# Seven block products for half of the last block's tails, and a copy moved to VectorE

## The chip, the cores and the metric

The kernel runs on one NeuronCore of a Trainium2 chip. The metric is the device time of one execution in microseconds (us). Before the change it was 275.11 us, the median of three runs (275.05 to 275.95). About 0.3% (0.8 us) is what a measurement of this kernel can tell from no change.

Engines: TensorE (PE in the profile, its weight loads PEld), VectorE (DVE), ScalarE (ACT), GpSimd (POOL), SyncE (SP, which only issues DMAs here). Each runs its own queue strictly in order and waits on semaphores for the others.

## The reference

Linear attention with cosine weights, then a two-layer network with a sigmoid-approximated gelu. For 8 batches of 8 heads, 576 positions and 64 features:

```
phi(x)  = [relu(x) * cos(pos), relu(x) * sin(pos)]
kv      = phi(k)^T v ;  z = sum over positions of phi(k)
attn    = (phi(q) kv) / (phi(q) z + 1e-6)
x       = attn as 4608 tokens of 512
h       = x @ w_in            (512 x 2048)
g       = h / (1 + exp(-1.702 h))
out     = g @ w_out           (2048 x 512)
```

Inputs and output are float32; the kernel computes the products in bf16 with sums in float32.

## The kernel before, in words

**Blocks and tails.** A batch has 576 tokens: a block of 512 and a tail of 64. The kernel runs batch by batch over the blocks; the tails' tokens are gathered in the tile `xt` (4 chunks of 128 features by 8 x 64 tokens). Batch 0's tail goes through the first product early (`mm1_tail_first`, result in `gt0`). The other seven tails, 448 tokens, are left for the last block, b = 7.

**The first product (x @ w_in)** has 16 groups of 128 hidden features, here numbered fc 0 to 15. Written plainly, one group is four matmuls (four chunks of features) into one PSUM bank and one gelu on ScalarE from that bank to SBUF. For the tails this is `mm1_tails` (L393 to L400): 64 matmuls of 448 columns, 16 gelus, the four banks of the pool `pmm` taken in turn. The gelu writes to `gt5`, the tile `gt` seen as 16 groups by 2 halves by 8 batches by 32 tokens: the first 32 tokens of every tail form one column half, the second 32 the other.

**Seven products for eight.** The larger products use the scheme of Strassen in Winograd's form: cut both matrices into 2 x 2 blocks, make a few sums of blocks, and do seven block products instead of eight. It is used twice.

- For the first product, a `Unit` (L643 to L695) does four groups fc (2u, 2u+1, 8+2u, 8+2u+1) for two column halves. It has seven steps, each of 4 matmuls: 1, 2, 6, 7, 5, 4, 3 in this order. Steps 1, 6, 7 and 4 add up in one bank (A), step 2 uses a second (Bk), steps 5 and 3 a third (Bp). After steps 1, 6 and 7 ScalarE copies bank A out to SBUF ("snap": s1, s2, s3, L672). VectorE adds such a copy to a bank (L667): c11 = s1 + step 2, c22 = s3 + step 5, c12 = s2 + (step 5 + step 3). Step 3 may only be added onto its bank when c22 has read it. Each of c11, c22, c12 and the end state of bank A gets a gelu on ScalarE.
- Weight sums (`win_sum`, L618 to L627: s1 to s4, in two halves of 512 columns each, "window sums" below, 128 x 1024 each) and x sums (`x_sum`, L632 to L641: t1, t2, t3, nt4) are made on VectorE ahead.
- For the second product (g @ w_out), `wino_mm` does the seven products of 16 matmuls each; the sums of g are made on VectorE by `g_sums` (L466 to L479), called "tail sums" when they are of the tails: s1 and s2 for two halves, then s3 and s4 for two halves, eight of 128 x 1024.

In blocks 2 to 6 a pair of units does half of the first product in the middle of seven plain groups (`mm1_pair`).

**The last block's order** (L1040 to L1113) is written out by hand, there is no scheduler; an engine's queue holds the instructions in the order in which the code emits them:

1. GpSimd: the copy of `gt0` into column 0 of `gt5` (L1041), then eight output DMAs that had been put off (`later`, L1043).
2. TensorE and ScalarE: `mm1_tails` for fc 0 to 15. VectorE meanwhile: eight window sums, four x sums.
3. VectorE: the tail sums s1, s2.
4. TensorE: four main units (the first product of block 7), with the 14 halves of the tails' second product between their steps: step 1 of unit 0, a half, step 2, a half, step 6, step 1 of unit 1, and so on. VectorE emits the tail sums s3, s4 after unit 0's c11.
5. The main block's second product, and its output.

The functions that the change touches and what calls them, with the line numbers of the profile:

Of the kernel before, what the change touches and what calls it, by code (L numbers as in the profile page):

```python
# [9 lines left out]
F32 = mybir.dt.float32  # L10
BF16 = mybir.dt.bfloat16
AF = mybir.ActivationFunctionType
# [3 lines left out]
SUB = mybir.AluOpType.subtract  # L16
# [4 lines left out]
def kernel(  # L21
# [9 lines left out]
    nc = tc.nc  # L31
    B, H, S, D = q.shape
# [3 lines left out]
    FC = d_ff // 128  # L36
    NS = S // 64
    MT = 512
# [8 lines left out]
    pmm = ctx.enter_context(tc.tile_pool(name="pmm", bufs=4, space=PSUM))  # L47
    pat = ctx.enter_context(tc.tile_pool(name="pat", bufs=2, space=PSUM))
# [61 lines left out]
    vt = one.tile([128, NS, NI, VW], BF16, name="vt")  # L110
# [257 lines left out]
    def gelu(fc, units=False):  # L368
        if fc % 4 == 0 and not units:
            gT[fc // 4] = gpool.tile([128, 4, MT], BF16, name="g")  # L370
        nc.scalar.activation(gT[fc // 4][:, fc % 4], hp.pop(fc), AF.Gelu_apprx_sigmoid)  # L371
# [18 lines left out]
                                 start=(kc == 0), stop=(kc == KC - 1))  # L390
        nc.scalar.activation(gt0[:, ts(half, 8)], hps, AF.Gelu_apprx_sigmoid)

    def mm1_tails(fc):  # L393
        hps = pmm.tile([128, MT], F32, name="mm")
        for kc in range(KC):
            nc.tensor.matmul(hps[:, 64:B * 64], wcol(kc, fc), xt[:, kc, 64:B * 64],  # L396
                             start=(kc == 0), stop=(kc == KC - 1))
        nc.scalar.activation(gt5[:, fc, :, 1:B].rearrange("p a b t -> p b a t"),
                             hps[:, 64:B * 64].rearrange("p (b a t) -> p b a t", a=2, t=32),
                             AF.Gelu_apprx_sigmoid)  # L400
# [210 lines left out]
    def slot():  # L611
        slot_no[0] += 1
        return slots[slot_no[0] % 8].rearrange("p (f t) -> p f t", f=2)

    def win_sum(n, i, ws=ws):
        tt = nc.vector.tensor_tensor
        o = {m: ws[m][:, :, ts(i, 512)] for m in ws}
        a = {(0, k): w_in_t[i][:, ts(k, 2), :] for k in range(2)}  # L618
        a.update({(1, k): w_in_t[2][:, ts(k, 2), ts(i, 512)] for k in range(2)})
        if n == "s1":  # L620
            tt(o[n], a[1, 0], a[1, 1], op=ADD)
        elif n == "s2":
            tt(o[n], o["s1"], a[0, 0], op=SUB)
        elif n == "s3":
            tt(o[n], a[0, 0], a[1, 0], op=SUB)
        else:
            tt(o[n], a[0, 1], o["s2"], op=SUB)  # L627

    def x_blk(b, k, t):
        return x[b][:, ts(k, 2), ts(t, 256)]  # L630

    def x_sum(b, n, xs=xs):  # L632
        tt = nc.vector.tensor_tensor
        if n == "t1":
            tt(xs[n], x_blk(b, 0, 1), x_blk(b, 0, 0), op=SUB)
        elif n == "t2":
            tt(xs[n], x_blk(b, 1, 1), xs["t1"], op=SUB)
        elif n == "t3":
            tt(xs[n], x_blk(b, 1, 1), x_blk(b, 0, 1), op=SUB)
        else:  # L640
            tt(xs[n], x_blk(b, 1, 0), xs["t2"], op=SUB)  # L641

    class Unit:  # L643
        def __init__(self, b, u, A, Bk, Bp, ws=ws, xs=xs, slot=slot):
            self.b, self.u, self.ws, self.xs, self.slot = b, u, ws, xs, slot
            self.A, self.Bk, self.Bp = [t.rearrange("p (f t) -> p f t", f=2) for t in (A, Bk, Bp)]

        def mm(self, to, a, t, opens):
            for j in range(2):
                fc = 2 * self.u + j  # L650
                for k in range(2):
                    if isinstance(a, str):
                        lhs = self.ws[a][:, k, ts(fc // 4, 512)].rearrange("p (f c) -> p f c", c=4)[:, :, fc % 4]
                    else:
                        lhs = wcol(2 * a[1] + k, 8 * a[0] + fc)
                    rhs = self.xs[t][:, k] if isinstance(t, str) else x_blk(self.b, *t)[:, k]

                    nc.tensor.matmul(to[:, j], lhs, rhs, start=(opens and j == 0 and k == 0), stop=(k == 1),  # L658
                                     skip_group_check=True)

        def gelu(self, f, t, i):
            o = gT[2 * f + self.u // 2][:, ds(2 * (self.u % 2), 2), ts(t, 256)]
# [12 lines left out]
        def step(self, p):  # L675
            if p == 1:
                self.mm(self.A, (0, 0), (0, 0), True)
                self.s1 = self.snap(self.A)
            elif p == 2:
                self.mm(self.Bk, (0, 1), (1, 0), True)  # L680
                self.c11 = self.add(self.s1, self.Bk)
            elif p == 6:
                self.mm(self.A, "s2", "t2", False)
                self.s2 = self.snap(self.A)
            elif p == 7:
                self.mm(self.A, "s3", "t3", False)
                self.s3 = self.snap(self.A)
            elif p == 5:
                self.mm(self.Bp, "s1", "t1", True)
                self.c22 = self.add(self.s3, self.Bp)  # L690
            elif p == 4:
                self.mm(self.A, (1, 1), "nt4", False)
            else:
                self.mm(self.Bp, "s4", (1, 1), False)
                self.c12 = self.add(self.s2, self.Bp)  # L695

# [13 lines left out]
    def x_pair(b):  # L712
        t = xpool.tile([128, KC, MT], BF16, name="xT")
        xp[b] = {n: t[:, i].rearrange("p (k t) -> p k t", k=2) for i, n in enumerate(("t1", "t2", "t3", "nt4"))}
        for n in xp[b]:
            x_sum(b, n, xp[b])
# [256 lines left out]
    for b in range(1, B):  # L973
        nb = b + 1 if b + 1 < B else None
        if nb is None:
            break
        f0 = 5 if b == 1 else 0
        if b in PAIR:
            mm1_pair(b, nb)
        for fc in range(f0, FC) if b not in PAIR else ():  # L980
            if b == 1 and fc == f0:
                for c in range(5):
                    trig_q(c)
                    qturn_dma(c)
            if nb is not None and fc == f0 + 1:
                kv_operands(nb)

                if nb + 1 < B:
                    load(kf, k, nb + 1, nc.sync)
                    load_q(nb + 1, nc.sync)  # L990
            if fc == 8 and b == 1:
                vcopy()
            if fc == 12:
                g_sums(("s1", "s2"), 0)
            mm1(b, fc)
        if nb is not None:
            x_open(nb)
            if b == 1:
                kv_mm_next()
            g_sums(("s1", "s2"), 1)  # L1000
            if b > 1:
                x_next(nb, 0)
            if b == 1:
                kv_evac(0, 4)
                g_sums(("s3",), 0)
            at = ({2: [0], 3: [1], 4: [2], 6: [3], 8: [4]} if b == 1 else
                  {s: [p + 1 if nb < B - 1 else (4, 1, 2, 3)[p]] for p, s in enumerate((1, 3, 4, 6))})
            wino_open()
            for p in range(7):
                for c in range(2):  # L1010
                    wino_mm(p, c)
                    s = 2 * p + c
                    if c == 1:
                        wino_after(b, p)
                    for c2 in at.get(s, ()):
                        x_next(nb, c2)
                        if c2 == 3 and nb + 1 < B:
                            load(vf, v, nb + 1, nc.sync)

                    s0 = 4 if b > 2 else 8  # L1020
                    if s0 <= s < s0 + 5 and nb + 1 < B:
                        trig_q(s - s0, act=True)
                    if 8 <= s < 13 and nb + 1 < B:
                        qturn_dma(s - 8)
                    if s == 4 and b > 1:
                        for n in ("s3", "s4"):
                            g_sums((n,), 0)
                            g_sums((n,), 1)
                    if s == 2 and b == 1:
                        g_sums(("s3",), 1)  # L1030
                    if s == 4 and b == 1:
                        g_sums(("s4",), 0)
                    if s == 6 and b == 1:
                        g_sums(("s4",), 1)
            if nb in PAIR:
                x_pair(nb)

    b = B - 1  # L1040
    nc.gpsimd.tensor_copy(gt5[:, :, :, 0], gt0.rearrange("p f (a t) -> p f a t", a=2))  # L1041
    for o, i in later:
        nc.gpsimd.dma_start(out=o, in_=i)  # L1043
    for fc in range(FC):
        mm1_tails(fc)
        if fc == 0:
            for n in ("s1", "s2", "s3", "s4"):
                for i in range(2):
                    win_sum(n, i)
            for n in ("t1", "t2", "t3", "nt4"):  # L1050
                x_sum(b, n)
    for h in range(2):
        g_sums(("s1", "s2"), h, TAIL)
    two = [pat.tile([128, 2, 512], F32, name="at") for _ in range(2)]
# [89 lines left out]
```

## Time and profile before

| what | value |
|---|---|
| median of three runs | 275.11 us |
| the profiled execution: time, span | 275.49 us, 273.4 us |
| granted TensorE clock | 0.998 |
| stage 2, tails' first product (L396) | 64 matmuls from 220.89 to 233.00 us |
| stage 4 | 233.00 to 257.49 us |
| stage 5 | from 257.49 us, TensorE's last matmul about 269.9 us |
| VectorE busy in 221 to 233 us | 7.95 of 12.0 us |
| ScalarE busy in 221 to 233 us | 8.76 of 12.0 us |
| VectorE busy in 233 to 257.6 us | 15.07 of 24.6 us |

How the lines are read. A line of the chain gives start, length, engine, what, source line, and how many instructions were merged. A line of the order of time gives start and length (us), engine, source line, operation, output tile <- input tiles, sizes, how many instructions were merged, and in brackets how long the engine had been idle and what ended that. A group line gives, behind the bar, the busy time in us, the mean of one instruction in ns, and the idle time before. Instructions of one engine overlap a little: the next one starts some 0.1 us before the last is over, so the price of one in a full queue is the distance of starts.

### The profile page before, as it was taken

To read this page: it belongs to the slowest core of one execution; us is meant where nothing else is said; L and a number is where in the kernel's file an instruction comes from. 1 tells how busy PE (TensorE), PEld (TensorE's weight loads), DVE (VectorE), ACT (ScalarE), POOL (GpSimd) and SP (SyncE) were. 2 spreads that over 40 slices of the span, in tenths; PEclk is the share of its full clock that TensorE was granted. 3 is DMA by queue.
4 is the path that set the end of the run, shared out by engine and by line. 5 is a ranking of instruction groups with operands and counts; after the bars stand their busy time and mean duration, and the time that the engine had idled before them with its cause. 6 is when DMAs were issued, how large, how long until landed. Compare 5 with 4: busy or idle time off the path is not lost.

```text
span 273.4 us, 7042 instructions
## 1 busy us (share of the span) xinstructions
PE 265.7 (97%) x2847; PEld 207.2 (76%) x2868; DVE 207.8 (76%) x487; ACT 174.8 (64%) x317; POOL 42.4 (15%) x71
## 2 busy tenths in 40 slices
PE   7899999999999999999999999999999999999994
PEld 2585645856987799778877887788778976999983
DVE  3956866698879798879887988888888994745741
ACT  5957642585199728983888387848783147677621
POOL 5691000000121012101110012001200173000410
PEclk9999999999999999999999999999999999999999
DMA  7999999999999996999898789796970654000333
GB/s 233 254 211 298 274 296 143 273 304 175 332 185 284 240 267 192 227 236 256 243 250 236 210 175 285 162 304 127 293 159 2 108 153 137 0 2 0 88 107 115
DMA packets 73663, 53.60 MB, mean 196 GB/s; under 512 B 52736, under 2 KB 63488, under 8 KB 73632
## 3 DMA queue, kind: packets, MB, share of 16 engines
q1 hardware_dynamic: 67504, 36.97, 58.3%
q0 software_dynamic: 6128, 16.19, 23.9%
q8 instruction: 22, 0.36, 0.6%
q14 instruction: 9, 0.07, 0.1%
HBM read 36.70 MB, written 9.44 MB: 169 GB/s over the span
## 4 chain that ended last, share of the span: by engine, by line
PE 93%; DMA 4%; DVE 1%; issue 1%; ACT 0%; POOL 0%
PE mm L520 31%; PE mm L658 16%; PE mm L365 13%; PE at L721 9%; PE mm L421 5%; PE at L520 4%; PE mm L396 4%; PE at L237 4%; PE at L310 3%; DMA sums<-in_v_dram 2%; DMA kf<-in_k_dram 1%; PE at L342 1%; PE mm L389 1%; DVE xn L325 1%; PE mm L205 0%
## 5 line engine op out<-in xcount | busy, mean ns | idle before, releaser
L520 PEld LDWEIGHTS <-sums 128*128 128x128 bf16 x448 | 42.5, 98 | 4.8
L526 POOL DMA_DIRECT2D out_dram<-ysb x24 | 17.4, 727 | 180.2 <-DVE inv L323 88.2
L520 PE MATMUL mm<-wsum,sums 128*128 128x256 bf16 x336 | 39.9, 272 | 0.0
L365 PE MATMUL mm<-xT,w_in 128*128 128x512 bf16 (+1 forms) x239 | 38.7, 305 | 0.5
L520 PEld LDWEIGHTS <-g 128*128 128x128 bf16 x336 | 32.0, 98 | 3.6
L371 ACT ACTIVATE g<-mm 128x512 bf16<-128x512 f32 x42 | 24.1, 598 | 10.9 <-PE mm L365 10.9
L365 PEld LDWEIGHTS <-w_in 128*128 128x128 bf16 x248 | 21.3, 114 | 11.5
L721 PE MATMUL at<-xT,w_in 128*128 128x512 bf16 x110 | 27.8, 379 | 0.5
L325 DVE TENSOR_TENSOR xn<-at,inv 128x512 bf16<-128x512 f32 x39 | 27.0, 691 | 1.3
L169 DVE TENSOR_SCALAR kr<-kf,cosw 128x256 bf16<-128x256 f32 x69 | 24.6, 357 | 3.0 <-DMA kf<-in_k_dram 3.0
L520 PE MATMUL mm<-w_out_sb,g 128*128 128x256 bf16 x224 | 26.6, 273 | 0.0
L169 DVE TENSOR_SCALAR kr<-kf,sinw 128x256 bf16<-128x256 f32 x68 | 23.6, 347 | 0.0
L658 PE MATMUL mm<-xT,w_in 128*128 128x256 bf16 x152 | 22.0, 273 | 0.0
L658 PE MATMUL mm<-xT,gt 128*128 128x256 bf16 x160 | 21.5, 272 | 0.0
L658 PEld LDWEIGHTS <-w_in 128*128 128x128 bf16 x168 | 18.6, 114 | 3.3
L183 ACT ACTIVATE qn<-qf,cosw 128x512 bf16<-128x512 f32 (+1 forms) x27 | 19.2, 711 | 1.5 <-DMA qf<-in_q_dram 1.1
L658 PEld LDWEIGHTS <-gt 128*128 128x128 bf16 x160 | 17.6, 113 | 3.0 <-issue 1.2
L721 PEld LDWEIGHTS <-w_in 128*128 128x128 bf16 x120 | 13.5, 113 | 8.2
L183 ACT ACTIVATE qn<-qf,sinw 128x512 bf16<-128x512 f32 (+1 forms) x27 | 19.2, 709 | 0.0
L371 ACT ACTIVATE g<-at 128x512 bf16<-128x512 f32 x30 | 17.5, 598 | 2.0 <-PE at L721 1.3
L535 ACT ACTIVATE kept_p<-mm 128x512 f32<-128x512 f32 (+1 forms) x15 | 8.5, 566 | 16.0 <-PE mm L520 16.0
L535 ACT ACTIVATE kept_u<-mm 128x512 f32<-128x512 f32 (+1 forms) x8 | 4.4, 544 | 20.6 <-PE mm L520 20.6
(175 smaller groups left out, 471.3 us busy)
## 6 DMA issues: line engine op xcount, KB each, us to landing
kf<-in_k_dram SPq DMA_DIRECT2D x6, 1152.0 KB, 9.2
vf<-in_v_dram SPq DMA_DIRECT2D x6, 1152.0 KB, 6.5
qf<-in_q_dram SPq DMA_DIRECT2D x6, 1024.0 KB, 6.3
out_dram<-ysb POOLq DMA_DIRECT2D x24, 256.0 KB, 5.1
w_out_sb<-in_moe_w_out_dram POOLq DMA_DIRECT2D x4, 512.0 KB, 17.7
kf<-in_k_dram POOLq DMA_DIRECT2D x1, 1152.0 KB, 13.4
vf<-in_v_dram POOLq DMA_DIRECT2D x1, 1152.0 KB, 20.8
w_in<-in_moe_w_in_dram POOLq DMA_DIRECT2D x2, 512.0 KB, 10.0
```

What stands on the lines that cost most here:

```text
L169: eng.tensor_scalar(o, i, 0.0, w[:, j:j + 1], op0=MAX, op1=MUL)
L183: nc.scalar.activation(o, i, AF.Relu, scale=sc)
L237: nc.tensor.matmul(st["kv", i][:, hh, ds(col, n)], kr[r, j, i, :], rhs(r, i, j), start=(j == 0), stop=(j == NS - 1))
L325: nc.vector.tensor_tensor(xn, pv[:, :, :, 0:64], inv.unsqueeze(3).to_broadcast([128, 2, 4, 64]), op=MUL)
L365: nc.tensor.matmul(hp[fc][:, t0:t1], wcol(kc, fc), x[b][:, kc, t0:t1], start=(kc == 0), stop=(kc == KC - 1))
L371: nc.scalar.activation(gT[fc // 4][:, fc % 4], hp.pop(fc), AF.Gelu_apprx_sigmoid)
L421: nc.tensor.matmul(yp[b, t, c0][:, c0:c1], w, w_out_sb[:, fc, c0:c1], start=(fc == 0), stop=(fc == FC - 1))
L520: nc.tensor.matmul(bank[to][c], lhs, rhs, start=opens, stop=(fc == HF - 1), skip_group_check=True)
L526: eng.dma_start(out=dst[:, 2 * i + c0:2 * i + c1, ts(n, HD)], in_=t[:, c0:c1])
L535: nc.scalar.activation(o, i, AF.Identity)
L658: nc.tensor.matmul(to[:, j], lhs, rhs, start=(opens and j == 0 and k == 0), stop=(k == 1), skip_group_check=True)
L721: nc.tensor.matmul(hp[fc], wcol(kc, fc), x[b][:, kc], start=(kc == 0), stop=(kc == KC - 1))
```

## The change

Half of the tails' first product (fc 0 to 3 and 8 to 11) is done by two units, `TailUnit` U and V, on the two column halves of 32 tokens of each of seven tails: 7 x 32 = 224 columns a matmul. The other eight groups (fc 4 to 7 and 12 to 15) stay plain; six of them use the pool `pat` (two double banks), the last two `pmm`. The order of steps is that of `mm1_pair`.

The window sums of the first half are emitted right behind block 6 with new x sums of the tails (`xt_sum`, into `vt`); those of the second half, the copy of `gt0` (now on VectorE) and the main block's x sums between the steps.

```diff
-    def mm1_tails(fc):
-        hps = pmm.tile([128, MT], F32, name="mm")
+    def mm1_tails(fc, at=False):
+        hps = pat.tile([128, 2, 512], F32, name="at")[:, 0] if at else pmm.tile([128, MT], F32, name="mm")
...
+    NT = (B - 1) * 32
+    xt5 = xt[:, :, 64:B * 64].rearrange("p k (b a t) -> p k a b t", a=2, t=32)
+    vt_flat = vt.rearrange("p j i e -> p (j i e)")
+    xs_tail = {n: vt_flat[:, ts(i, 2 * NT)].rearrange("p (k b t) -> p k b t", k=2, t=32)
+               for i, n in enumerate(("t1", "t2", "t3", "nt4"))}
+
+    def xt_sum(n):
+        tt = nc.vector.tensor_tensor
+        blk = {(k, a): xt5[:, ts(k, 2), a] for k in range(2) for a in range(2)}
+        o = xs_tail
+        if n == "t1":
+            tt(o[n], blk[0, 1], blk[0, 0], op=SUB)
...
+    class TailUnit(Unit):
+        def __init__(self, u, A, Bk, Bp):
+            Unit.__init__(self, B - 1, u, A, Bk, Bp, ws, None, lambda: slot()[:, :, 0:NT])
+            self.A, self.Bk, self.Bp = [t[:, :, 0:NT] for t in (self.A, self.Bk, self.Bp)]
+
+        def rhs(self, t, k):
+            if isinstance(t, str):
+                return xs_tail[t][:, k]
+            return xt5[:, 2 * t[0] + k, t[1]]
+
+        def gelu(self, f, t, i):
+            fc = 8 * f + 2 * self.u
+            nc.scalar.activation(gt5[:, fc:fc + 2, t, 1:B], i.rearrange("p f (b t) -> p f b t", t=32),
+                                 AF.Gelu_apprx_sigmoid)
...
+            if nb == B - 1:
+                for k in range(2):
+                    win_sum(("s1", "s2")[k], 0)
+                for k in range(2):
+                    xt_sum(("t1", "t2")[k])
+                for k in range(2):
+                    win_sum(("s3", "s4")[k], 0)
+                    xt_sum(("t3", "nt4")[k])
...
     b = B - 1
-    nc.gpsimd.tensor_copy(gt5[:, :, :, 0], gt0.rearrange("p f (a t) -> p f a t", a=2))
     for o, i in later:
         nc.gpsimd.dma_start(out=o, in_=i)
-    for fc in range(FC):
-        mm1_tails(fc)
-        if fc == 0:
-            for n in ("s1", "s2", "s3", "s4"):
-                for i in range(2):
-                    win_sum(n, i)
-            for n in ("t1", "t2", "t3", "nt4"):
-                x_sum(b, n)
+    banks4 = [pmm.tile([128, 512], F32, name="mm") for _ in range(4)]
+    U, V = [TailUnit(u, banks4[u], banks4[2], banks4[3]) for u in range(2)]
+    U.step(1)
+    V.step(1)
+    mm1_tails(4, True)
+    mm1_tails(5, True)
+    U.step(2)
+    U.step(6)
+    V.step(6)
+    U.gelu(0, 0, U.c11)
+    mm1_tails(6, True)
+    mm1_tails(7, True)
+    V.step(2)
+    U.step(7)
+    U.step(5)
+    V.gelu(0, 0, V.c11)
+    for n in ("s1", "s2"):
+        win_sum(n, 1)
+    V.step(7)
+    mm1_tails(12, True)
+    U.gelu(1, 1, U.c22)
+    U.step(4)
+    U.gelu(1, 0, U.A)
+    U.step(3)
+    for n in ("s3", "s4"):
+        win_sum(n, 1)
+    V.step(4)
+    V.gelu(1, 0, V.A)
+    U.gelu(0, 1, U.c12)
+    mm1_tails(13, True)
+    V.step(5)
+    nc.vector.tensor_copy(gt5[:, :, :, 0], gt0.rearrange("p f (a t) -> p f a t", a=2))
+    for n in ("t1", "t2", "t3", "nt4"):
+        x_sum(b, n)
+    mm1_tails(14)
+    V.gelu(1, 1, V.c22)
+    V.step(3)
+    V.gelu(0, 1, V.c12)
+    mm1_tails(15)
     for h in range(2):
         g_sums(("s1", "s2"), h, TAIL)
```

More of the change, by code (lines that the diff above doesn't have):

```diff
@@ L655, in mm @@
                         lhs = wcol(2 * a[1] + k, 8 * a[0] + fc)
-                    rhs = self.xs[t][:, k] if isinstance(t, str) else x_blk(self.b, *t)[:, k]
+                    rhs = self.rhs(t, k)
                     nc.tensor.matmul(to[:, j], lhs, rhs, start=(opens and j == 0 and k == 0), stop=(k == 1),
                                      skip_group_check=True)
+        def rhs(self, t, k):
+            return self.xs[t][:, k] if isinstance(t, str) else x_blk(self.b, *t)[:, k]
         def gelu(self, f, t, i):
@@ L695, in step, with rhs @@
                 self.c12 = self.add(self.s2, self.Bp)
+    NT = (B - 1) * 32
[9 more added lines that the diff above has]
+            tt(o[n], blk[0, 1], blk[0, 0], op=SUB)
+        elif n == "t2":
+            tt(o[n], blk[1, 1], o["t1"], op=SUB)
+        elif n == "t3":
+            tt(o[n], blk[1, 1], blk[0, 1], op=SUB)
+        else:
+            tt(o[n], blk[1, 0], o["t2"], op=SUB)
+    class TailUnit(Unit):
+        def __init__(self, u, A, Bk, Bp):
+            Unit.__init__(self, B - 1, u, A, Bk, Bp, ws, None, lambda: slot()[:, :, 0:NT])
+            self.A, self.Bk, self.Bp = [t[:, :, 0:NT] for t in (self.A, self.Bk, self.Bp)]
+        def rhs(self, t, k):
+            if isinstance(t, str):
[5 more added lines that the diff above has]
+                                 AF.Gelu_apprx_sigmoid)
     PAIR = range(2, B - 1)
```

## Prediction

> **What bounds the kernel now.** I read the page's busy shares first, then the chain that ended last, then the groups of TensorE by shape, and last the order of time on VectorE, ScalarE and TensorE around 221 to 241 us.
>
> ```profile
> PE 265.7 (97%) x2847; PEld 207.2 (76%) x2868; DVE 207.8 (76%) x487; ACT 174.8 (64%) x317; POOL 42.4 (15%) x71
> ```
>
> ```profile
> 221.06 12.11 PE mm L396 x64
> ...
> 257.65 12.24 PE mm L520 x112
> ```
>
> ```profile
> L396 PE MATMUL mm<-xt,w_in 128*128 128x448 bf16 x64 | 12.3, 352 | 0.0
> ...
> L389 PE MATMUL mm<-xt,w_in 128*128 128x64 bf16 x64 | 2.3, 198 | 0.0
> ```
>
> TensorE is the bound. The chain of the last block is TensorE without a gap: the tails' first product (L396, 64 matmuls in 12.11 us, 0.1892 each), the main units mixed with the tails' second product, then the main block's second product (112 in 12.24, 0.1093 each). What is saved in L396 is saved in the end only if TensorE stays without gaps behind it.
>
> ```profile
> 230.82 0.69 DVE L473 TENSOR_TENSOR kr<-gt 128x1024 bf16<-128x1024 bf16 x1 [3.22 <-ACT gt L398]
> 231.54 0.69 DVE L475 TENSOR_TENSOR kr<-kr,gt 128x1024 bf16<-128x1024 bf16 x1
> 233.78 0.69 DVE L473 TENSOR_TENSOR kr<-gt 128x1024 bf16<-128x1024 bf16 x1 [1.54 <-ACT gt L398]
> 234.50 0.69 DVE L475 TENSOR_TENSOR kr<-kr,gt 128x1024 bf16<-128x1024 bf16 x1
> 235.11 0.68 DVE L667 TENSOR_TENSOR qn<-qn,mm 128x512 f32<-128x512 f32 x1
> 235.71 1.28 DVE L477 TENSOR_TENSOR qT<-gt 128x1024 bf16<-128x1024 bf16 x2
> 236.91 1.28 DVE L479 TENSOR_TENSOR qT<-gt,kr 128x1024 bf16<-128x1024 bf16 x2
> 238.51 0.69 DVE L667 TENSOR_TENSOR qf<-qn,mm 128x512 f32<-128x512 f32 x1 [0.31 <-PE mm L658]
> 239.11 0.68 DVE L667 TENSOR_TENSOR qf<-qf,mm 128x512 f32<-128x512 f32 x1
> ```
>
> ```profile
> 239.55 0.60 PE L658 MATMUL mm<-qf,w_in 128*128 128x256 bf16 x4
> 239.99 0.49 PE L658 MATMUL mm<-xT,vf 128*128 128x256 bf16 x3
> ```
>
> This is the place that decides. VectorE waits 3.22 and 1.54 us for the tails' gelus, but from 233.78 on it is busy without a gap but 0.31 us: tail sums, main unit 0's c11 (235.11), four tail sums, unit 1's c11 (238.51), unit 0's c22 (239.11). TensorE's step 3 of unit 0 (239.99) adds onto the bank that c22 reads and must wait for it. A sum is over about 0.71 us after its start (0.60 until the next starts, and 0.11 more until a dependent one can: 234.50 follows 233.78 by 0.72), so c22 is done at 239.82. **The slack is 0.2 us.** Whatever delays VectorE's queue by more stops TensorE.
>
> ```profile
> 236.37 1.08 ACT L672 ACTIVATE qn<-mm 128x512 f32<-128x512 f32 x2
> 237.33 0.64 ACT L663 ACTIVATE g<-qn 128x512 bf16<-128x512 f32 x1
> 238.00 0.60 ACT L672 ACTIVATE qf<-mm 128x512 f32<-128x512 f32 x1
> ```
>
> ScalarE starts a PSUM read of 512 every 0.48 us (two from 236.37 to 237.33); a gelu from SBUF is 0.04 longer.
>
> ```profile
> 222.36 1.96 DVE L625 TENSOR_TENSOR vf<-w_in,w_in 128x1024 bf16<-128x1024 bf16 x1
> ...
> 222.72 1.05 POOL L1041 COPY gt<-gt 128x1024 bf16<-128x1024 bf16 x1
> ```
>
> Beside GpSimd's copy one window sum takes 1.96 us instead of 0.69.
>
> **The change part by part.**
>
> *TensorE.* Removed: 32 of 64 matmuls of 448, 32 x 0.1892 = 6.05 us. Added: 56 of 224. From 0.1093 at 256 and 0.1892 at 448 a column costs 0.416 ns, so one of 224 takes 0.096 and all 5.38. **Gain 0.68.** Weight loads set no floor: the 64 matmuls of 64 columns (L389), with the same strided weights, pass in 2.3 us, 0.036 each. The page "TensorE: Matmul & The Clock Gate" of the Trainium skill, section "LDWEIGHTS (loading the stationary operand)", gives columns / 1.2 ns, 107 ns for 128, which as a floor would make the 56 take 5.99 and leave a gain of 0.06; the L389 row is against it. 24 of the 56 read xt directly in runs of 32 tokens, which no row shows. From below: no cost, as for the same tile read whole. From above: half rate, 24 x 0.096 = 2.3 us. I take none, since only the step between runs is new.
>
> *ScalarE.* 8 of 16 gelus go (0.544 long each); 6 copies out and 8 gelus come, all of 448. At 0.43 a start from PSUM (0.485 less the 0.054 by which 448 is shorter than 512) and 0.47 from SBUF, 22 make about 9.7 us in 12: no bound of its own, but its queue keeps order, see below.
>
> *GpSimd.* The copy leaves; the row output DMAs behind it are issued 1 us earlier, and nothing waits for them until the tails' results. VectorE gets back the 1.3 us of L625, worth nothing there: it idled 3.22 us later in that stage.
>
> *VectorE.* The eight window sums (0.60 each) and four x sums (0.34, the second 0.45 as it depends on the first) stay. New: four x sums of 448 (0.30 estimated; as slow as one f32 element stream, 0.53, they still end before step 6 needs them), six sums from PSUM of 448 (0.60 at 512 less 64 columns: 0.535), and the copy of 1024 bf16 values. The copy's price is not in the trace: the nearest row is the bf16 sum of 1024 at 0.60, which I take; from below 0.33 (half the stream), from above 1.17 (the rate of f32 sums from PSUM, 0.60 for 512, doubled less a start). The Trainium skill, "VectorE: DVE Perf Modes", section "The perf-mode tier table", puts bf16 copies at twice the rate of tensor_tensor; by that it would be the lower end and the sum 1.47 instead of 1.74. No row here shows such a copy.
>
> **The path.** I walked the three queues in the changed program's order from 220.89, each instruction starting when its queue is free and its operands are there (TensorE's result seen 0.20 after the last issue, as 233.00 + 0.44 to ScalarE's 233.64; ScalarE's 0.14 and VectorE's 0.11 after the next could start). The same walk over the order before gives TensorE 233.00, 235.62, 237.37 and 239.99 as in the trace.
>
> TensorE runs free until V's step 5 (230.04). V's c22 waits for it and for U's c12 and the two window sums s3, s4 ahead in VectorE's queue: 230.96 to 231.60, and V's step 3 on the same bank stands 0.42 us. Then in VectorE's queue come the copy (0.60) and the four x sums (1.45) **ahead of V's c12**, which step 3 had ready at 232.2 and which starts at 233.54. Behind c12's gelu (234.19) ScalarE, idle for 1.9 us, holds gelu 15 and the copy out of main unit 0 (235.09), so unit 0's step 6 stands 0.35 us, to 235.72. The first tail sum needs V's c12 gelu: 234.80 instead of 230.82, so that all four tail sums now lie in one row ahead of unit 0's c11. On VectorE:
>
> - 230.96 + c22 0.535 + copy 0.60 + x sums 1.45 = 233.54
> - + c12 0.645 + its gelu 0.615 = 234.80
> - + four tail sums 0.71 + 0.60 + 0.71 + 0.60 = 237.42 (unit 0's c11, before 235.11; unit 1's step 2 stands 0.23 for it)
> - + c11 0.60 + four tail sums 2.40 + unit 1's c11 0.60 = 241.02 (unit 0's c22, before 239.11)
> - + 0.71 = 241.73, when unit 0's step 3 can start; before 239.99.
>
> **Sum:** 241.73 - 239.99 = **+1.74 us**; by TensorE: -0.68 + 0.42 + 0.35 + 0.23 + 1.42 = 1.74. Behind it VectorE idles again (2.9 us before the next c11), so nothing more is lost and nothing won back: TensorE has no gap to give. The profiled execution took 275.49 (span 273.4), 0.38 over the median of 275.11; it becomes 277.2, the median **276.85**.
>
> With every open VectorE price at its low end the walk gives +1.05, at its high end with a slightly dearer matmul (0.107) +2.75. That is the likeliest case's own range: 276.2 to 277.9.
>
> **The rivals.**
>
> *VectorE keeps up (faster).* If the sums of 1024 passed faster than 0.60, the queue would be empty before c22 of unit 0. For: L625 shows that GpSimd's copy held VectorE, and it is gone. Against: every other row of that shape, with GpSimd idle or issuing DMAs, is 0.60 or 0.72. It decides from 0.45 with the copy at 0.33 (-0.06); with both at 0.33 it is -0.51: 274.6, and 0.17 of TensorE's gain is still lost.
>
> *The lateness is half hidden (no change).* Prices below the low ends, or a copy and x sums that start in a gap I don't see: without the copy alone the path is 0.60 shorter, without copy and x sums the loss is about 0.4. Within 0.3% (0.8 us, about what a measurement of this kernel can tell) I put 275.6.
>
> *Strided xt is slow.* At half rate for the 24 matmuls the walk gives +3.55: 278.7. For it: no row shows runs of 32 into TensorE. Against: ScalarE writes such runs at its usual 0.544.
>
> *The weight load as floor* of 0.107 (the Trainium skill's rule above) would be +2.10, 277.2; it lies within the likeliest case's range, and L389 speaks against it.
>
> **How the numbers follow.** Likeliest case 0.74, faster 0.06, no change 0.11, slow xt 0.09. Predicted 276.9. The range of 275.8 to 278.1 leaves out the faster case, some of the no-change case and the slow xt. Faster by over 0.3%: 0.06; within: 0.11; slower: 0.83.
>
> **What would show it.** Right: L658 with 128x224 at 0.096 apart; the tails' product ends (start of unit 0's step 1) near 232.7, 0.3 earlier than 233.00; V's c12 starts over 1 us after its matmuls; ScalarE idles nearly 2 us before its gelu; unit 0's c22 near 241; and one TensorE gap of over 1 us ahead of unit 0's step 3. Wrong: no such gap (VectorE's prices), or 224 columns over 0.11 apart (xt or weights), or a copy far from 0.6.

## The result and the profile after

The changed kernel takes **276.51 us** (median of six runs, 276.28 to 276.60) against 275.10 us before: 1.41 us more, ratio 1.0047 with a 95% interval of 1.0035 to 1.0060. It is slower, as forecast, and lies in the range; the point was 276.9.

The profiled execution took 276.53 us with a span of 274.6, 1.2 us more than the span before. The last block alone lost more: from the start of the tails' first product to the start of the main block's second product it took 38.17 us (220.43 to 258.60) instead of 36.60 (220.89 to 257.49), **+1.57**. The profiled execution reached that stage 0.46 us earlier than before, since the first load of k took 3.38 us here and 3.90 in the profile of before, which is no work of the change. Below, runs are compared by this stretch, so that the first load does not blur them.

The chain that ended last in the changed kernel, in order of time (start, length, engine, tile, line):

```profile
231.13 0.34 DVE gt L1120
231.47 0.34 DVE qf L635
231.84 0.42 DVE qf L637
...
232.93 0.54 DVE qn L670
233.50 0.59 ACT gt L732
234.11 0.70 DVE kr L473
234.84 0.69 DVE kr L475
235.53 0.61 DVE kr L473
236.16 0.03 DVE kr L475
236.20 0.57 issue
236.77 0.69 DVE qf L670
...
239.86 1.21 DVE qn L670 x2
241.06 0.04 issue
241.11 0.60 PE mm L658 x4
```

What was TensorE from end to end before is now mainly VectorE for ten microseconds: copy, x sums, V's c12, one gelu on ScalarE, then tail sums and unit 0's c11 up to unit 0's c22.

TensorE by shape (busy, mean, idle before), then TensorE in order of time around the largest gap:

```profile
L658 PE MATMUL mm<-xt,w_in 128*128 128x224 bf16 x16 | 2.0, 259 | 0.0
L658 PE MATMUL mm<-vt,kf 128*128 128x224 bf16 x16 | 2.0, 259 | 0.0
```

```profile
239.25 0.60 PE L658 MATMUL mm<-qf,w_in 128*128 128x256 bf16 x4
241.11 0.60 PE L658 MATMUL mm<-xT,vf 128*128 128x256 bf16 x4 [1.26 <-DVE qn L670]
```

Matmuls that read `xt` in runs of 32 tokens are as fast as those that read the sums in one piece. Eight that read `xt` pass in 0.77 us (220.43 to 221.20), 0.096 each, and so do two steps of four, one of either kind (227.66 to 228.43). The tails' product took 11.89 us to the start of unit 0's step 1 (232.32), 0.47 of it a gap, against 12.11 before, so that the matmuls alone are 0.69 shorter. The four of 239.25 are issued by 239.69; the next start at 241.11, 1.42 later.

ScalarE and VectorE, in order of time:

```profile
231.35 0.57 ACT L732 ACTIVATE gt<-qn 128x448 bf16<-128x448 f32 x1
233.50 0.58 ACT L732 ACTIVATE gt<-qn 128x448 bf16<-128x448 f32 x1 [1.57 <-DVE qn L670]
233.98 0.53 ACT L398 ACTIVATE gt<-mm 128x448 bf16<-128x448 f32 x1
234.41 0.59 ACT L675 ACTIVATE qf<-mm 128x512 f32<-128x512 f32 x1
```

```profile
230.52 0.61 DVE L670 TENSOR_TENSOR qn<-qn,mm 128x448 f32<-128x448 f32 x1
231.05 0.42 DVE L1120 COPY gt<-gt 128x1024 bf16<-128x1024 bf16 x1
231.39 0.42 DVE L635 TENSOR_TENSOR qf<-xT 128x512 bf16<-128x512 bf16 x1
231.84 0.42 DVE L637 TENSOR_TENSOR qf<-xT,qf 128x512 bf16<-128x512 bf16 x1
232.18 0.42 DVE L639 TENSOR_TENSOR qf<-xT 128x512 bf16<-128x512 bf16 x1
232.52 0.42 DVE L641 TENSOR_TENSOR qf<-xT,qf 128x512 bf16<-128x512 bf16 x1
232.85 0.61 DVE L670 TENSOR_TENSOR qn<-qf,mm 128x448 f32<-128x448 f32 x1
234.11 0.69 DVE L473 TENSOR_TENSOR kr<-gt 128x1024 bf16<-128x1024 bf16 x1 [0.65 <-ACT gt L732]
...
240.38 0.68 DVE L670 TENSOR_TENSOR qn<-qn,mm 128x512 f32<-128x512 f32 x1
```

ScalarE stands 1.57 us ahead of the gelu of V's c12 (233.50). The first tail sum waits for that gelu and starts at 234.11, 13.68 us into the stretch, where it had started 9.93 in before (230.82). Unit 0's c22 is the last line. The copy holds the queue for 0.34 us (231.05 to 231.39), not 0.60.

### The profile page after: what moved, and what is told of

It reads as the page before. It is cut to its first block, busy times and chain, and to the rows that moved or that the text cites. A ratio compares the mean times of both kernels' runs of the same rounds, so it can differ in the third digit from the quotient of the medians.

```text
span 274.6 us, 7113 instructions
## 1 busy us (share of the span) xinstructions
PE 265.6 (97%) x2871; PEld 208.8 (76%) x2892; DVE 211.4 (77%) x498; ACT 176.9 (64%) x323; POOL 41.4 (15%) x70
## 4 chain that ended last, share of the span: by engine, by line
PE 88%; DVE 5%; DMA 4%; issue 1%; ACT 1%; DVEq 0%; POOL 0%
PE mm L520 31%; PE mm L658 16%; PE mm L365 13%; PE at L759 9%; PE mm L421 5%; PE at L237 4%; PE at L310 3%; PE at L520 3%; DMA sums<-in_v_dram 2%; DVE qn L670 1%; DMA kf<-in_k_dram 1%; PE at L396 1%; PE at L342 1%; PE mm L389 1%; DVE xn L325 1%
## 5 line engine op out<-in xcount | busy, mean ns | idle before, releaser
L365 PEld LDWEIGHTS <-w_in 128*128 128x128 bf16 x248 | 21.3, 114 | 11.5
L658 PEld LDWEIGHTS <-w_in 128*128 128x128 bf16 x192 | 21.0, 114 | 4.1 <-issue 0.3
L759 PEld LDWEIGHTS <-w_in 128*128 128x128 bf16 x120 | 13.5, 113 | 8.2
```

What stands on the lines that cost most here:

```text
L365: nc.tensor.matmul(hp[fc][:, t0:t1], wcol(kc, fc), x[b][:, kc, t0:t1], start=(kc == 0), stop=(kc == KC - 1))
L759: nc.tensor.matmul(hp[fc], wcol(kc, fc), x[b][:, kc], start=(kc == 0), stop=(kc == KC - 1))
```

## Experiments

In each, the ratio is to the kernel before, run beside it, with its 95% interval, and the stretch is the one above (before 36.60, the change 38.17). A TensorE gap is a start less the issue end of what came ahead, worked out from the starts as for 239.25 above. With the change the gaps are 0.47 (V's step 3), 0.10 (unit 0's step 6), 0.28 (unit 1's step 2) and 1.42 (unit 0's step 3), 2.27 in all, against a shorter product; 2.27 - 1.57 leaves a gain of 0.70 for that, beside the 0.69 read directly.

Theory 1 is the prediction's: VectorE's queue is a full row from V's c22 to unit 0's c22, and its total work counts (with one wait in it, for the gelu of V's c12). Theory 2: the loss hangs on V's c12 standing behind the copy and the x sums. Theory 3: the units as such cost the time.

**The copy and x sums behind c12.**

```diff
     V.step(5)
-    nc.vector.tensor_copy(gt5[:, :, :, 0], gt0.rearrange("p f (a t) -> p f a t", a=2))
-    for n in ("t1", "t2", "t3", "nt4"):
-        x_sum(b, n)
     mm1_tails(14)
     V.gelu(1, 1, V.c22)
     V.step(3)
+    nc.vector.tensor_copy(gt5[:, :, :, 0], gt0.rearrange("p f (a t) -> p f a t", a=2))
+    for n in ("t1", "t2", "t3", "nt4"):
+        x_sum(b, n)
```

> The copy and the four x sums are emitted behind V's c12 instead of ahead of it; nothing else. Theory 1 (VectorE's queue is full from V's c22 to main unit 0's c22, so that only the sum of its work counts): nothing gained, +1.4 us against the kernel before, as with the change; c12 starts 1.3 us earlier, but the first tail sum starts where it did (within 0.2 us), as it now comes behind the copy and x sums, and the gap ahead of unit 0's step 3 stays 1.4 us. Theory 2 (the loss comes from c12's place behind the copy and x sums, which holds ScalarE's queue): 1.3 us or more of the loss goes, the time is the kernel before's +0.1 us or less.

Ratio 1.0048 (1.0025 to 1.0071); stretch 38.17, to the hundredth that of the change. VectorE in this run, in order of time:

```profile
232.95 0.62 DVE L670 TENSOR_TENSOR qn<-qf,mm 128x448 f32<-128x448 f32 x1 [0.63 <-PE mm L658]
233.49 0.42 DVE L1123 COPY gt<-gt 128x1024 bf16<-128x1024 bf16 x1
...
234.95 0.42 DVE L641 TENSOR_TENSOR qf<-xT,qf 128x512 bf16<-128x512 bf16 x1
235.29 0.68 DVE L473 TENSOR_TENSOR kr<-gt 128x1024 bf16<-128x1024 bf16 x1
```

c12 starts 11.34 us into the stretch (which began at 221.61) instead of 12.42, 1.1 earlier where 1.3 was expected. The first tail sum starts 13.68 in, and so it did with the change. What was saved by c12 was paid behind it, and the gap of 1.42 stayed. That it is the same to the hundredth rests on two waits of like length: with the change VectorE stands 0.65 us for the gelu of V's c12 (ahead of 234.11), here 0.63 us for V's step 3 (ahead of 232.95), and the copy and x sums run while that gelu does. So the row is not busy throughout; it holds about 0.65 us of waiting in either order. Theory 2 as it stands, by which over 1.3 us would have gone, falls: the wait of ScalarE in the profile is real, but to move c12 ahead does not shorten the row.

**The copy and x sums where VectorE stood idle.**

```diff
     U.step(2)
+    nc.vector.tensor_copy(gt5[:, :, :, 0], gt0.rearrange("p f (a t) -> p f a t", a=2))
+    for n in ("t1", "t2", "t3", "nt4"):
+        x_sum(b, n)
     U.step(6)
...
     V.step(5)
-    nc.vector.tensor_copy(gt5[:, :, :, 0], gt0.rearrange("p f (a t) -> p f a t", a=2))
-    for n in ("t1", "t2", "t3", "nt4"):
-        x_sum(b, n)
```

> The copy and the four x sums are emitted right behind U's c11, where VectorE stood idle 2.06 us ahead of V's c11. Theory 1: VectorE's full row is 1.8 us shorter, but VectorE then waits 0.7 us for the gelu of V's c12; unit 0's step 3 waits about 0.6 us instead of 1.4, the other gaps of the main units go, V's step 3 still waits 0.4: +0.4 us against the kernel before. Theory 2: as in theory 1, c12 is on time: +0.1 us or less. Theory 3 (the units themselves cost the time, by shorter matmuls and the longer ScalarE queue): still +1.2 us or more.

Ratio 1.0012 (0.9999 to 1.0025); stretch 37.10, +0.50. TensorE at unit 0's step 3:

```profile
239.59 0.60 PE L658 MATMUL mm<-qf,w_in 128*128 128x256 bf16 x4
240.75 0.60 PE L658 MATMUL mm<-xT,vf 128*128 128x256 bf16 x4 [0.56 <-DVE qn L670]
```

The gap is 0.72 instead of 1.42, those at unit 0's step 6 and unit 1's step 2 are gone, V's step 3 still waits 0.48. By theory 1 it was +0.4, by theory 2 at most +0.1, by theory 3 at least +1.2. The time alone (0.0 to 0.7 us more than before) rules out theory 3 only; against theory 2 speaks the stretch. Of the 1.8 us moved away, 1.07 came back, since VectorE now waits both for V's step 3 and for the gelu of c12 (0.64 us each).

**Four tail sums later.**

```diff
-        if (p, c) == (0, 1):
+        if (p, c) == (2, 0):
             for n in ("s3", "s4"):
                 for h in range(2):
                     g_sums((n,), h, TAIL)
```

> The change as it is, but the tail sums s3 and s4 (four of 0.60 us) are emitted behind unit 0's c12 (behind the third product's first half) instead of behind unit 0's c11. Theory 1: the gap of 1.4 us ahead of unit 0's step 3 goes, the smaller ones (0.47, 0.10, 0.28) stay: +0.1 us against the kernel before. Theory 2: c12's place is unchanged, so the loss stays: +1.2 us or more. Theory 3: +1.2 us or more.

Ratio 1.0014 (0.9996 to 1.0033); stretch 36.76, +0.16. c12 stands behind copy and x sums as ever, but TensorE passes unit 0's step 3 without waiting:

```profile
239.43 0.60 PE L658 MATMUL mm<-qf,w_in 128*128 128x256 bf16 x4
239.86 0.60 PE L658 MATMUL mm<-xT,vf 128*128 128x256 bf16 x4
```

By the stretch, nine tenths of the loss go by a move that touches nothing of the product that was changed; the other gaps (0.47, 0.10, 0.27) are as they were. The time, 0.1 us less to 0.9 more than before, is blurred but below the +1.2 of theories 2 and 3. Both fall here.

**More work in the row.** First, a window sum is repeated:

```diff
     for n in ("t1", "t2", "t3", "nt4"):
         x_sum(b, n)
+    win_sum("s4", 1)
     mm1_tails(14)
```

> One window sum of 128x1024 (0.60 us) is made a second time, between the x sums and V's c12. Theory 1: the row is full, so the time grows by just this 0.60 us over the change, +2.0 us against the kernel before, and the added wait shows at unit 0's step 6 (0.1 becomes 0.7). Theory 3: VectorE is not the bound and nothing changes: +1.4 us.

Ratio 1.0129 (1.0105 to 1.0153), far more than 0.60 us over the change. The stretch is 39.44, 1.27 over the change; the rest of the profiled execution's excess, 0.63, lies ahead of the stretch. TensorE shows what went otherwise than expected:

```profile
231.81 0.26 PE L658 MATMUL mm<-xt,vf 128*128 128x224 bf16 x1 [0.31 <-DVE qn L670]
234.22 0.48 PE L658 MATMUL mm<-xt,vf 128*128 128x224 bf16 x3 [2.15 <-DVE vf L627]
```

V's step 3 reads the first half of s4 from `vf`, and the repeat rewrites the second half in the same rows: three of the step's four matmuls waited for it, and it stands behind the copy and the x sums. c12 came later by that. So this run has a new wait of its own and decides nothing about the row. Next, an x sum is repeated on a tile that no step waits for there:

```diff
     for n in ("t1", "t2", "t3", "nt4"):
         x_sum(b, n)
+    for _ in range(2):
+        x_sum(b, "nt4")
     mm1_tails(14)
```

> The last x sum is made two more times (0.34 us each) between the x sums and V's c12, on a tile that no step waits for there. Theory 1: the row is full, the time grows by these 0.68 us over the change, and all of it shows ahead of unit 0's step 6 (0.1 becomes 0.8). Theory 3: nothing changes.

Ratio 1.0090 (1.0073 to 1.0107); stretch 39.10, 0.93 over the change. The two took 0.92 on VectorE (from the start of V's c22 to that of c12 3.25 us, with the change 2.33), about 0.45 each and not 0.34; each rewrites what the one ahead wrote, and 0.45 is also what the x sum takes that reads what the one ahead wrote (231.39 to 231.84). All of it stands ahead of unit 0's step 6, which is held through ScalarE's queue:

```profile
234.11 1.04 PE L520 MATMUL at<-w_out_sb,gt 128*128 128x256 bf16 x8
236.01 0.49 PE L658 MATMUL mm<-qf,kf 128*128 128x256 bf16 x3 [0.86 <-ACT qf L675]
```

234.11 + 0.88 = 234.99, so 1.02 instead of 0.10. A microsecond more in this row is a microsecond in the end: the expected size was off, by the price of the repeated sum, the mechanism not.

**The copy alone.** The kernel before with only this line of the change:

```diff
-    nc.gpsimd.tensor_copy(gt5[:, :, :, 0], gt0.rearrange("p f (a t) -> p f a t", a=2))
+    nc.vector.tensor_copy(gt5[:, :, :, 0], gt0.rearrange("p f (a t) -> p f a t", a=2))
```

> The kernel before with the copy of batch 0's tails on VectorE, nothing else of the change. Theory 1: no change (within 0.2 us): VectorE pays 0.34 us and gets back the 1.3 us by which GpSimd's copy lengthened one window sum, and both fall in front of its 3.2 us of idling; the window sum is back at 0.69 us. Rival: if the copy on VectorE did delay the end, or the lengthened sum had cost time before, the time would move by 0.3 us or more.

Ratio 1.0003 (0.9993 to 1.0013), stretch 36.59: no change. Each window sum takes 0.69 us, and VectorE idles 4.09 us ahead of the first tail sum instead of 3.22, so that the time that it got back went into idling. And the change with the copy left on GpSimd, ahead of the output DMAs:

> The change with the copy left on GpSimd, at its old place. Theory 1: VectorE's full row is 0.34 us shorter, but one window sum is lengthened by 1.3 us again, now with U's c11 behind it: +1.3 to +1.4 us against the kernel before, nearly as with the change. Rival (the copy on VectorE is a main part of the loss): +1.0 us or less.

Ratio 1.0054 (1.0034 to 1.0073), stretch 37.94, +1.34. Where the copy runs is no main part of the loss: net 0.23 of the 1.57. In this run GpSimd's copy met another sum:

```profile
223.20 1.42 DVE L716 TENSOR_TENSOR vt<-xt 128x448 bf16<-128x448 bf16 x1
...
223.31 1.05 POOL L1087 COPY gt<-gt 128x1024 bf16<-128x1024 bf16 x1
```

The same sum takes 0.38 us with GpSimd idle; here it is over only after the copy.

**All three moves.** Copy and x sums behind U's c11, the tail sums s3 and s4 behind unit 0's c12, and window sum s4 of the second half behind V's c12, so that V's c22 is on time:

```diff
     U.step(2)
+    nc.vector.tensor_copy(gt5[:, :, :, 0], gt0.rearrange("p f (a t) -> p f a t", a=2))
+    for n in ("t1", "t2", "t3", "nt4"):
+        x_sum(b, n)
...
-    for n in ("s3", "s4"):
-        win_sum(n, 1)
+    win_sum("s3", 1)
...
     V.step(5)
-    nc.vector.tensor_copy(gt5[:, :, :, 0], gt0.rearrange("p f (a t) -> p f a t", a=2))
-    for n in ("t1", "t2", "t3", "nt4"):
-        x_sum(b, n)
...
     V.step(3)
+    win_sum("s4", 1)
...
-        if (p, c) == (0, 1):
+        if (p, c) == (2, 0):
```

> Three moves on VectorE at once, with the units kept: copy and x sums right behind U's c11, the second half's window sum s4 behind V's c12, the tail sums s3 and s4 behind unit 0's c12. Theory 1: no TensorE gap over 0.1 us is left in the last block, the main block's second product starts 36.0 us after the start of the tails' first product (36.60 before, 38.17 with the change), and the time is 0.6 us below the kernel before. Theory 3 (the units themselves cost time): not below the kernel before.

**274.59 us, ratio 0.9971 (0.9959 to 0.9982): faster than both kernels.** The stretch is 36.09, 0.51 below the kernel before; of the shorter product's 0.70 only V's step 3 takes 0.18 back, where no gap over 0.1 was expected. V's c22 starts there 0.27 us after the last matmul of V's step 5 is issued (230.08 to 230.35), so little of that wait is left to VectorE's queue. VectorE and TensorE at the place that decides:

```profile
235.53 0.68 DVE L670 TENSOR_TENSOR qf<-qf,mm 128x512 f32<-128x512 f32 x1
237.67 0.69 DVE L670 TENSOR_TENSOR qn<-qn,mm 128x512 f32<-128x512 f32 x1 [1.46 <-PE mm L658]
```

```profile
238.71 0.60 PE L658 MATMUL mm<-qf,w_in 128*128 128x256 bf16 x4
239.15 0.60 PE L658 MATMUL mm<-xT,vf 128*128 128x256 bf16 x4
```

VectorE now idles 1.46 us between unit 0's c11 and unit 1's, and TensorE runs through.

To see whether that gain is the units' or the later tail sums', the latter alone in the kernel before (the same edit as in "four tail sums later"):

> The kernel before, without units, with the tail sums s3 and s4 behind unit 0's c12 as in the best version. If the gain of the best version is the units' shorter product (theory 1), this move alone gives nothing, as the kernel before had no TensorE gap there: the main block's second product starts 36.6 us after the tails' first product, the time is unchanged within 0.2 us. If the kernel before already lost time to VectorE's queue, this alone would be faster by up to 0.6 us.

Ratio 1.0004 (0.9992 to 1.0015), stretch 36.59: nothing. The kernel before had no gap there to close, so the gain is the units'. In the change as it stood, the waits for VectorE took more than that gain.

## Why the prediction was right

Step by step, in the block:

| step of the prediction | forecast | measured |
|---|---|---|
| a matmul of 224 columns | 0.096 us | 0.096 |
| gain of the tails' first product | 0.68 | 0.70 |
| strided reads of `xt` | no cost | no cost |
| the copy in VectorE's queue | 0.60 (0.33 to 1.17) | 0.34 |
| V's step 3 waits for c22 | 0.42 | 0.47 |
| unit 0's step 6 waits | 0.35 | 0.10 |
| unit 1's step 2 waits | 0.23 | 0.28 |
| unit 0's step 3 waits for c22 | 1.42 | 1.42 |
| sum in the block | +1.74 | +1.57 |

The likeliest case came true in every step but one size: **the copy**, taken at the price of a sum of two tensors, cost 0.34 and so lay at the lower end that was kept. The difference went almost whole into unit 0's step 6, whose wait is 0.25 shorter than forecast. The prediction had named a copy far from 0.6 as a sign of being wrong, and that sign came; it was worth 0.25 of the 1.74 us, and the other terms stood without it. The page "VectorE: DVE Perf Modes" of the Trainium skill ("The perf-mode tier table") puts bf16 copies at twice the rate of sums. The trace comes close to it, 0.34 us a start against 0.60 for 1024 values, here even with a target in runs of 32 values. With the low price the walk gave +1.47; the 0.10 up to the measured 1.57 are mostly the waits at V's step 3 and unit 1's step 2, 0.05 longer each.

The other signs came as named: V's c12 starts 1.28 us after its matmuls are issued (231.57 to 232.85), ScalarE idles 1.57 us ahead of its gelu (nearly 2 with the dear copy), and one gap of over 1 us stands ahead of unit 0's step 3.

The rival "VectorE keeps up" falls with the rows of the tail sums, 0.60 to 0.73 from start to start, which are as before. "Half hidden" falls with the repeated x sum: the row gave nothing of it back. The weight load as a floor (the Trainium skill's "TensorE: Matmul & The Clock Gate", "LDWEIGHTS (loading the stationary operand)") falls with 0.096 a matmul, below the 0.107 that it would set.

One thing the prediction's list of waits does not tell, and the moves do: the four waits have not four causes. The first, at V's step 3, hangs on the window sum ahead of c22: it stays at 0.48 when copy and x sums are moved and falls to 0.18 when window sum s4 is. The other three are one late row that shows at whichever step meets it: with c12 moved, the wait at step 6 goes and that at unit 1's step 2 grows from 0.28 to 0.34.

That the measured time (+1.41) is a little below the block's +1.57 is within the interval of the ratio (0.96 to 1.65 us).

## What to carry to other kernels

Before shortening work on the bounding engine, list what the engines beside it must do in the shorter time, in queue order, up to the next place where the bounding engine waits for them, and compare that sum with the slack there; here it was 0.2 us of slack against a row that ended 1.7 us later (unit 0's c22 starts 19.95 us into the stretch, before 18.22). An idle share of a stage (VectorE was busy 8 of 12 us) does not show that; the same work put into the idle piece, and sums that are needed late taken out of the row, turned a loss of 1.4 us into a gain of 0.7. And moving the late instruction forward in the same row changed here which wait was seen, not when the row ended.

## What the hardware showed beyond that

- In these traces a VectorE sum that reads or rewrites what the one ahead wrote starts 0.11 us later: 0.45 instead of 0.34 for 128x512, 0.72 instead of 0.60 for 128x1024.
- Twice a VectorE sum of two SBUF tensors started just ahead of a GpSimd copy (by 0.11 and 0.36 us) and ended after it: it took 1.42 us instead of 0.38 with the change, and 1.96 instead of 0.69 in the kernel before.
- In the run with the repeated window sum, a write to the other half of a weight sum's tile held three matmuls for 2.15 us, most of it the time until the 0.60 us sum had its turn in VectorE's queue. No run shows whether the hardware needs this wait or only the program sets it.
